# Attention scores computed in one tile mode, with the mask moved out of the memory queries' matmuls and the instruction order refitted

## Chip, cores, metric

One core of one Trainium2 chip. The metric is device time in microseconds (us) of one launch, lower is better. Runs of the kernel before on several chips lie between 2154 and 2166 us. Every run whose state is on record was in the fast state, so the comparisons below are of fast runs with fast runs.

## The reference

A sequence of 2048 tokens of width 576 goes through four residual layers: A (windowed attention, 32 heads of 18), B (32 heads of 128, segments of 32 tokens with 8 memory tokens that one segment hands to the next), then A and B again. The change touches B alone:

```python
for s in range(n_seg):                       # 64 segments of 32
    h = jnp.concatenate([mem, xs], axis=1)   # 8 memory rows, 32 x rows
    q, k, v = h @ Wq, h @ Wk, h @ Wv         # (cut: per head, 32 heads of 128)
    scores = jnp.einsum('bhqe,bhke->bhqk', q, k) * scale
    scores = jnp.where(mask, scores, -1e9)   # memory queries see all 40 keys;
                                             # x queries see memory and earlier x
    p = softmax(scores); o = p @ v; o = o @ Wo
    mem = o[:, :M]; outs.append(o[:, M:])
```

The memory makes each B layer a chain of 64 steps. The kernel runs the two B layers as two **lanes**, the second five steps behind the first, so that one step computes 80 rows: 32 x rows and 8 memory rows of each lane. The A layers' tiles of 64 tokens are fitted between.

## The kernel before

The program isn't written in the order in which it runs. Each piece of work is an operation with an engine, an estimated duration, a priority and its dependencies. A planner in the kernel simulates the engines with those durations and emits instructions in the order that it finds. Its settings (`PR`) were fitted to the durations beforehand. **New durations or settings mean a new order.** The planner also has a model of instruction fetch, with one constant time:

```python
    LAT = {"PE": 0.22, "ACT": 0.08, "DVE": 0.08, "POOL": 0.08, "SP": 2.8, "NONE": 0.0}
    SWITCH = 0.1                                    # a change of TensorE's tile mode
    PAGE, AHEAD, FETCH, POS = 256, 64, 4.1, 63
    ...                                             # (cut) in fetched(), at each block border:
                avail = max(avail, t0 + (t1 - t0) * (page - self.AHEAD - p0) / (p1 - p0)) + self.FETCH
```

A block of 256 instructions is taken to be asked for 320 instructions before it starts (64 before the block ahead of it), and to be usable 4.1 us later.

The scores of 16 heads, twice a step:

```python
            for v, msk in ((m, self.mask_m[:].unsqueeze(1).to_broadcast([P, 4, W80])),
                           (x, self.mask_x[:].unsqueeze(2).to_broadcast([P, 2, 4, 48]))):
                nc.tensor.matmul(v, lhsT=self.ident4[:], rhs=msk, start=True, stop=False, skip_group_check=True)
            for i in range(4):                      # memory queries: four heads side by side in column tiles
                for c in range(4):
                    h = heads[i][c]
                    nc.tensor.matmul(m[c * 32:(c + 1) * 32, i, :], lhsT=q(h, MC, 32), rhs=k(h, 0, W80), start=False, stop=True, ...)
            for l in range(2):                      # x queries of each lane
                for i in range(4):
                    for c in range(4 if on[l] else 0):
                        h = heads[i][c]
                        nc.tensor.matmul(x[c * 32:(c + 1) * 32, l, i, :], lhsT=q(h, XC[l], 32), rhs=k(h, KX[l], 48), start=False, ...)
```

The two mask matmuls use the full array, the scores four column tiles. After them come the softmax on VectorE, ScalarE and GpSimd (`amax`, `Exp`, `norm`, `mult`), the value products in row tiles (`pv`, 48 matmuls), and the output projection (`oproj`, 160 matmuls on the full array, in operations of 20).

The A layers' weights don't fit on the core beside B's. Tile by tile they are loaded again into a ring of buffers, by SyncE's DMA queue, up to 320 KB each:

```python
        def fetch(e):                               # in wload(); i >= 9: the A output weights
            dma(out=w.t[:, 0:5 * n], in_=self.strips[i][:, 0:5 * n])
```

## Time and profile before

| | before |
|---|---|
| time, median of 3 runs | 2161.72 us (2159.29 to 2165.41) |
| span of the profiled execution | 2165.8 us |
| TensorE busy | 2061.8 us, 95% |
| VectorE, ScalarE, GpSimd busy | 64%, 54%, 43% |
| ring loads | 488 of 320 KB, median 3.4 us from issue to landing; 244 of 160 KB, 3.9 us |
| instruction packets (16 KB, 256 instructions) | 472 |

Read it so: TensorE is nearly always busy and the others are not, so a change pays if it takes work from TensorE or closes holes between its matmuls. The prediction below shows the lines.

### The profile page before, as it was taken

The numbers are of one execution on the slowest core, as the hardware profiler recorded it, in microseconds if no ns is written. First come the engines' busy times: TensorE is split into PE (matmuls) and PEld (weight loads), VectorE is DVE, ScalarE is ACT, GpSimd is POOL, SyncE is SP. The second block draws the span as 40 slices with busy tenths as digits, with TensorE's granted clock in tenths as the row PEclk, the third lists the DMA queues.
The fourth block names the chain that finished last, engine by engine and source line by source line (L and its number), as shares of the span: only waits on it lengthen the run. The fifth ranks groups of instructions, "written<-read, shape, count | busy, mean of one in ns | idle before, by whom it ended". The sixth has DMA issues, their size and how long they took to land.

```text
span 2165.8 us, 132233 instructions
## 1 busy us (share of the span) xinstructions
PE 2061.8 (95%) x60441; PEld 1727.4 (80%) x60441; DVE 1392.3 (64%) x3525; ACT 1169.7 (54%) x2859; POOL 937.7 (43%) x1325
## 2 busy tenths in 40 slices
PE   2698999999999999999999999999999999999997
PEld 2476888888888888888888888888888888888876
DVE  4466766666666666666666666666666666765675
ACT  2244555555556555555555555555555555655543
POOL 3145444454444544445444454444445445442220
PEclk9799999999999999999999999999999999999999
DMA  9654334343344343334333343333344434332110
GB/s 324 184 155 138 119 108 122 120 131 118 120 125 125 115 128 119 122 119 130 120 115 119 121 135 111 123 122 117 115 132 127 121 112 130 118 119 92 59 57 10
DMA packets 158305, 265.11 MB, mean 122 GB/s; under 512 B 23464, under 2 KB 89904, under 8 KB 157616
## 3 DMA queue, kind: packets, MB, share of 16 engines
q1 hardware_dynamic: 152016, 237.38, 35.8%
q0 software_dynamic: 4576, 18.88, 2.5%
q8 instruction: 472, 7.73, 1.5%
q14 instruction: 89, 0.73, 0.1%
q10 hardware_dynamic: 1152, 0.39, 0.1%
HBM read 240.46 MB, written 16.12 MB: 118 GB/s over the span
## 4 chain that ended last, share of the span: by engine, by line
PE 92%; DMA 4%; DVE 1%; issue 1%; ACT 1%; SPq 0%; POOL 0%; ACTq 0%; POOLq 0%
PE r L833 28%; PE r L987 18%; PE r L880 17%; PE r L573 7%; PE r L836 6%; PE r L963 3%; PE r L683 2%; PE r L912 2%; PE r L473 2%; PE r L916 2%; PE r L647 1%; PE r L922 1%; DMA ring<-strip 1%; DMA ring<-in_A_wqkv_dram 1%; PE r L622 1%
## 5 line engine op out<-in xcount | busy, mean ns | idle before, releaser
L833 PE MATMUL r<-hT,wq 128*128 128x80 bf16 (+1 forms) x8832 | 660.0, 198 | 6.9 <-issue 3.0
L833 PE MATMUL r<-hT,wk 128*128 128x80 bf16 (+1 forms) x8832 | 662.5, 199 | 1.6 <-issue 1.5
L833 PEld LDWEIGHTS <-wq 128*128 128x128 bf16 x8832 | 499.9, 98 | 33.6 <-issue 23.7
L836 PE MATMUL r<-hT,wqk_r 128*128 128x160 bf16 (+1 forms) x2208 | 507.2, 230 | 0.2 <-issue 0.2
L275 ACT ACTIVATE qk<-r 128x480 bf16<-128x480 f32 (+3 forms) x659 | 345.7, 529 | 244.6 <-PE r L836 230.8
L833 PEld LDWEIGHTS <-wk 128*128 128x128 bf16 x8832 | 447.5, 99 | 2.2 <-issue 2.2
L987 PE MATMUL r<-OT,wo 128*128 128x80 bf16 (+1 forms) x11040 | 415.8, 200 | 16.7 <-issue 10.8
L987 PEld LDWEIGHTS <-wo 128*128 128x128 bf16 x11040 | 393.9, 99 | 32.6 <-issue 22.5
L880 PE MATMUL r<-wv,hT 128*32 128x512 bf16 x5376 | 354.5, 382 | 0.0
L282 POOL TENSOR_TENSOR big<-qT,kT 128x1024 bf16<-128x1024 bf16 x188 | 314.3, 1691 | 60.4 <-ACT kT L275 51.9
L282 POOL TENSOR_TENSOR ex<-ex,sum 128x384 bf16<-128x384 bf16 x137 | 116.7, 852 | 468.4 <-DVE sum L782 360.7
L282 POOL TENSOR_TENSOR big<-big 128x1280 bf16<-128x1280 bf16 (+1 forms) x61 | 123.0, 2016 | 422.2 <-DVE big L282 403.6
L880 PEld LDWEIGHTS <-hT 128*32 128x32 bf16 x6720 | 166.2, 96 | 127.1 <-issue 2.6
L275 ACT ACTIVATE V<-r 128x512 bf16<-128x512 f32 x301 | 179.6, 597 | 157.8 <-PE r L880 154.9
L771 DVE TENSOR_REDUCE nmx<-r 128x4 f32<-128x320 f32 (+1 forms) x276 | 143.2, 519 | 163.7 <-PE r L916 162.6
L836 PEld LDWEIGHTS <-wqk_r 128*128 128x128 bf16 x2208 | 219.7, 99 | 0.3 <-issue 0.3
L573 PE MATMUL r<-xn,ring 128*128 128x64 bf16 x4725 | 185.7, 194 | 23.1 <-DMA ring<-in_A_wqkv_dram 18.7
L573 PEld LDWEIGHTS <-ring 128*128 128x128 bf16 x4725 | 161.5, 98 | 44.4 <-DMA ring<-in_A_wqkv_dram 19.9
L275 ACT ACTIVATE OT<-r 128x320 bf16<-128x320 f32 (+1 forms) x375 | 137.5, 425 | 103.8 <-PE r L963 103.3
L275 ACT ACTIVATE big<-r 128x384 bf16<-128x384 f32 (+1 forms) x289 | 110.4, 443 | 88.8 <-issue 65.6
L772 DVE TENSOR_TENSOR r<-r,nmx 128x320 f32<-128x320 f32 (+1 forms) x276 | 147.2, 533 | 9.4
L880 PE MATMUL r<-wv_r,hT 128*32 128x512 bf16 x1344 | 133.4, 380 | 0.0
(150 smaller groups left out, 2906.3 us busy)
## 6 DMA issues: line engine op xcount, KB each, us to landing
ring<-strip SPq DMA_DIRECT2D x488, 320.0 KB, 3.4
ring<-strip SPq DMA_DIRECT2D x244, 160.0 KB, 3.9
x1T<-x SPq DMA_DIRECT2D x32, 160.0 KB, 4.4
x<-x1T SPq DMA_DIRECT2D x32, 160.0 KB, 4.3
x3T<-x SPq DMA_DIRECT2D x32, 160.0 KB, 4.4
x<-x3T SPq DMA_DIRECT2D x32, 160.0 KB, 4.3
wo<-in_B_Wo_dram POOLq DMA_DIRECT2D x4, 1152.0 KB, 30.6
wq<-in_B_Wq_dram POOLq DMA_DIRECT2D x2, 2048.0 KB, 20.6
```

What stands on the lines that cost most here:

```text
L275: nc.scalar.activation(out=out, in_=in_, func=ACT.Copy, scale=1.0 if scale is None else scale)
L282: (self.nc.vector if e == "DVE" else self.nc.gpsimd).tensor_tensor(out=out, in0=in0, in1=in1, op=op)
L473: nc.tensor.matmul(psf, lhsT=(self.ones if c < 4 else self.ones_h)[:, :], rhs=xs.t[:, c].rearrange("p a t -> p (a t)"), start=(c == 0), st ...
L573: nc.tensor.matmul(ps.t[:, c * T:(c + 1) * T], lhsT=view()[:, kc, w0:w0 + P], rhs=xn.t[:, kc, :], start=(kc == 0), stop=(kc == 4))
L683: nc.tensor.matmul(ps.t[:, mb * T:(mb + 1) * T], lhsT=view()[:, c, w0:w0 + P], rhs=oT.t[:, c, :], start=(c == 0), stop=(c == 4))
L771: nc.vector.tensor_reduce(out=m, in_=v, axis=AX.X, op=ALU.max, negate=True)
L772: nc.vector.tensor_tensor(out=v, in0=v, in1=m.unsqueeze(len(shp) - 1).to_broadcast(shp), op=ALU.add)
L833: nc.tensor.matmul(pv[:, hh, wi, a:b], lhsT=self.Wb[wi][0][:, kc, h * P:(h + 1) * P], rhs=hT.t[:, kc, a:b], start=(hh == 0 and wi == 0 and ...
L836: nc.tensor.matmul(pv[:, hh, :, a:b], lhsT=self.Wb[0][1][:, h * P:(h + 1) * P], rhs=hT.t[:, 4:6, a:b], start=False, stop=(hh == n - 1), sk ...
L880: nc.tensor.matmul(ps.t[c * 32:(c + 1) * 32, :], lhsT=l, rhs=w, start=(kc == 0), stop=(kc == 4))
L963: nc.tensor.matmul(ps[c].t[:, i * n + a - c0:i * n + z - c0], lhsT=V[b].t[q4, r, i, :], rhs=pt.t[q4, i, b, a:z], start=(i == 0 and b == bl ...
L987: nc.tensor.matmul(psY.t[:, mb * W80 + c0:mb * W80 + c1], lhsT=self.wo[:, w0:w0 + P], rhs=self.OT[:, h % 16 // 4 * 8 + h // 16 * 4 + h % 4 ...
```

## The change

**Intent.** Keep the scores block in one tile mode. The memory queries get no mask: each query sees the keys of both lanes, and after the softmax's sums the reciprocal of the other lane's sum is set to zero by a multiply with an ownership table. The x queries' mask, now on 40 keys instead of 48, is added by four column-tiled matmuls. Then durations and settings were fitted again, which gives a new order of the whole program. The core of the diff:

```diff
-KX = (0, 32)
+KX = (0, 40)
+KL = SEG + NM
...
-        self.mask_m = mk = cp.tile([P, W80], BF16, name="mask_m")
+        self.own_m = om = cp.tile([P, 4, 2], F32, name="own_m")
+        nc.gpsimd.memset(om[0:32], 1.0)
+        self.sel(om[0:32, :, 0], [[0, 4]], -1, NM - 1, ALU.is_ge, 0.0)
+        self.sel(om[0:32, :, 1], [[0, 4]], 1, -NM, ALU.is_ge, 0.0)
...
             nc.vector.reciprocal(out=s, in_=s)
-        o = pl.op("DVE", 0.69, norm, prio, [o], acq=[ss], uses=[e_])
+            if acq:
+                nc.vector.tensor_tensor(out=s, in0=s, in1=self.own_m[:], op=ALU.mult)
+        o = pl.op("DVE", 0.87 if acq else 0.69, norm, prio, [o], acq=[ss], uses=[e_])
...
-                nc.tensor.matmul(v, lhsT=self.ident4[:], rhs=msk, start=True, stop=False, skip_group_check=True)
+            for c in range(4):
+                q4 = slice(c * 32, (c + 1) * 32)
+                v, msk = (own(x, c * 32, 32, 0, NM, SEG), own_x) if all(on) else (x[q4], mx.unsqueeze(2).to_broadcast([P, 2, 4, KL]))
+                nc.tensor.matmul(v, lhsT=self.ident[:, 0:32], rhs=msk, start=True, stop=False, skip_group_check=True)
...
-        o = pl.op("PE", 0.68 if all(on) else 0.56, mm, prio, [self.qk_ev[g] for g in gs], acq=[psm, psx, em, ex],
+        o = pl.op("PE", 0.5 if all(on) else 0.39, mm, prio, [self.qk_ev[g] for g in gs], acq=[psm, psx, em, ex],
...
-PR = dict(qk=0.388, qkd=0.053, v1=1.358, v0=0.674, w=-0.059, s0=0.001, s1=-1.032, p0=1.109, p1=-0.981, o=0.434,
+PR = dict(qk=(0.121, -0.204), qkd=(0.07, 0.15), v1=(3.035, 1.45), v0=(5.889, 14.703), s0=(-0.83, 0.204), s1=(-7.824, -0.786), p0=(-5.413,
```

Cut: the views on 320 columns, small corrections of other durations, and the rest of the settings (a pair of values for even and odd steps where there was one).

More of the change, by code (lines that the diff above doesn't have):

```diff
@@ L60 @@
     LAT = {"PE": 0.22, "ACT": 0.08, "DVE": 0.08, "POOL": 0.08, "SP": 2.8, "NONE": 0.0}
-    SWITCH = 0.1
+    SWITCH = 0.097
     PAGE, AHEAD, FETCH, POS = 256, 64, 4.1, 63
@@ L160, in run @@
                             continue
-                        if alt is not None and o.prio > alt.prio + PR["w"]:
+                        if alt is not None and o.prio > alt.prio + PR["w" + mode]:
                             skipped.append(it)
@@ L299, in setup @@
         self.sel(ident[:], [[-1, P]], 1, 0, ALU.is_equal, 0.0)
-        self.ident4 = ident4 = cp.tile([P, P], BF16, name="ident4")
         self.ones = ones = cp.tile([P, P], BF16, name="ones")
@@ L322, in setup @@
         self.sel(ma0[:], [[ADIL, AW], [1, 16]], 0, -HALO, ALU.is_ge, NEG)
-        self.mask_m = mk = cp.tile([P, W80], BF16, name="mask_m")
-        nc.gpsimd.memset(mk[:], 0.0)
-        self.sel(mk[:, 40:80], [[0, 40]], 1, -NM, ALU.is_ge, NEG)
-        self.sel(mk[:, 0:40], [[0, 40]], -1, NM - 1, ALU.is_ge, NEG)
-        self.sel(mk[:, 0:40], [[0, 40]], -1, 2 * NM - 1, ALU.is_ge, 0.0)
-        self.mask_x = mx = cp.tile([P, 2, 48], BF16, name="mask_x")
+        self.own_m = om = cp.tile([P, 4, 2], F32, name="own_m")
+        nc.gpsimd.memset(om[0:32], 1.0)
+        self.sel(om[0:32, :, 0], [[0, 4]], -1, NM - 1, ALU.is_ge, 0.0)
+        self.sel(om[0:32, :, 1], [[0, 4]], 1, -NM, ALU.is_ge, 0.0)
+        self.mask_x = mx = cp.tile([P, 2, KL], BF16, name="mask_x")
         nc.gpsimd.memset(mx[:], 0.0)
-        nc.gpsimd.memset(mx[:, 0, 40:48], NEG)
-        nc.gpsimd.memset(mx[:, 1, 0:8], NEG)
-        self.sel(mx[:, 0, 0:32], [[-1, SEG]], 1, 0, ALU.is_ge, NEG)
-        self.sel(mx[:, 1, 16:48], [[-1, SEG]], 1, 0, ALU.is_ge, NEG)
+        self.sel(mx[:, 0, 0:SEG], [[-1, SEG]], 1, 0, ALU.is_ge, NEG)
+        self.sel(mx[:, 1, NM:KL], [[-1, SEG]], 1, 0, ALU.is_ge, NEG)
         self.Wb = []
@@ L397, in setup @@
         nc.vector.memset(wo[:, 11 * 1280:12 * 1280], 0.0)
-        nc.vector.tensor_copy(out=ident4[:].rearrange("p (a b) -> p a b", a=4), in_=ident[:, 0:32].unsqueeze(1).to_broadcast([P, 4, 32]))
         nc.vector.memset(mem0T[:], 0.0)
@@ L403, in setup @@
             nc.vector.tensor_copy(out=epadT[q4 * AH:(q4 + 1) * AH], in_=et)
+            nc.vector.tensor_copy(out=self.own_m[q4 * 32:(q4 + 1) * 32], in_=self.own_m[0:32])
         pp = self.pool("psum", 1, space=PSUM)
@@ L526, in pr @@
             return due - span * (1.0 - f)
-        Q = PR["A"]
+        Q = PR[f"A{layer}"]
         if layer == 1:
@@ L567, in a_tile @@
                     n = 256 if c < 4 else P
-                    view, w, ow = self.wload(part * 3 + c // 2, self.A_wqkv, (P, 512), part * D + CB[c], n, pr(Q[1]) - PR["ring"], wgate)
+                    view, w, ow = self.wload(part * 3 + c // 2, self.A_wqkv, (P, 512), part * D + CB[c], n, pr(Q[1]) - PR[f"ring{layer}"], wgate)
                 w0 = c % 2 * CB[1]
@@ L574, in mm @@
                                          start=(kc == 0), stop=(kc == 4))
-                o = pl.op("PE", 0.15, mm, pr(Q[1] + 0.03 * part), [o, ow], acq=[ps, dst[part]] if c == 0 else (),
+                o = pl.op("PE", 0.146, mm, pr(Q[1] + 0.03 * part), [o, ow], acq=[ps, dst[part]] if c == 0 else (),
                           uses=[xn, *w] if c == 0 else [xn, *w, ps], lat=0.0 if c < 4 else None, mm=5)
@@ L623, in logits @@
                                      start=(c == 0), stop=(c == 4))
-        o = o_l = pl.op("PE", 0.4, logits, pr(Q[3]), [o], acq=[psL, e_], uses=[big], mode="C", mm=20)
+        o = o_l = pl.op("PE", 0.29, logits, pr(Q[3]), [o], acq=[psL, e_], uses=[big], mode="C", mm=20)
         def amax(e):
@@ L652, in a_tile @@
             ps = [pl.buf("r") for _ in range(NQ)]
-            b = pl.op("PE", 0.09 * nb, lambda e, ps=ps, c0=c0, nb=nb: spread(ps, c0, nb), pr(Q[4] + 0.02 * n), [b], acq=ps,
+            b = pl.op("PE", 0.03 + 0.05 * nb, lambda e, ps=ps, c0=c0, nb=nb: spread(ps, c0, nb), pr(Q[4] + 0.02 * n), [b], acq=ps,
                       uses=[e_], mode="R", mm=4 * nb)
@@ L677, in a_tile @@
                 n = 256 if mb < 4 else P
-                view, w, ow = self.wload(9 + mb // 2, self.A_wo, (CB[1], CB[4]), mb * P, n, pr(Q[6]) - PR["ring"], o_l)
+                view, w, ow = self.wload(9 + mb // 2, self.A_wo, (CB[1], CB[4]), mb * P, n, pr(Q[6]) - PR[f"ring{layer}"], o_l)
             w0 = mb % 2 * P
@@ L683, in mm @@
                     nc.tensor.matmul(ps.t[:, mb * T:(mb + 1) * T], lhsT=view()[:, c, w0:w0 + P], rhs=oT.t[:, c, :], start=(c == 0), stop=(c == 4))
-            o = pl.op("PE", 0.15, mm, pr(Q[6]), [o, ow], acq=[ps] if mb == 0 else (),
+            o = pl.op("PE", 0.147, mm, pr(Q[6]), [o, ow], acq=[ps] if mb == 0 else (),
                       uses=[oT, *w] if mb == 0 else [oT, *w, ps], lat=0.0 if mb < 4 else None, mm=5)
@@ L797, in load_x @@
         self.hT[t] = hT
-        gate = pl.op("NONE", 0.0, None, t - 0.42, [self.qk_op.get(t - 1)], acq=[hT])
+        gate = pl.op("NONE", 0.0, None, t + PR["lx"], [self.qk_op.get(t - 1)], acq=[hT])
         self.x_in[t] = {l: gate for l in range(2)}
@@ L807, in load_x @@
                                     lambda e, l=l, s=s, xnb=xnb: self.copy(e, hT.t[:, :, XC[l]:XC[l] + SEG], xnb.t[:, s % NS]),
-                                    t - 0.42, [dep, gate], uses=[hT, xnb])
+                                    t + PR["lx"], [dep, gate], uses=[hT, xnb])
             if l == 0 and t % 2 == 0:
@@ L811, in load_x @@
                                      lambda e, s=s, xnb=xnb: self.copy(e, hT.t[:, :, W80:HW_], xnb.t[:, s % NS + 1, :, 0:HW_ - W80]),
-                                     t - 0.42, [dep, gate], uses=[hT, xnb])
+                                     t + PR["lx"], [dep, gate], uses=[hT, xnb])
             if s == 0:
@@ L837, in mm @@
                                  start=False, stop=(hh == n - 1), skip_group_check=True)
-        o = pl.op("PE", 0.0003 + (0.356 if b - a == W80 else 0.275) * n, mm, prio, [*self.x_in[t].values(), *self.mem_in[t]] + ([self.w_in[wi][n_] for wi in range(2) for n_ in
+        o = pl.op("PE", (0.356 if b - a == W80 else 0.275) * n, mm, prio, [*self.x_in[t].values(), *self.mem_in[t]] + ([self.w_in[wi][n_] for wi in range(2) for n_ in
                   {h // 16 for h in heads}] if t == 0 else []), acq=[ps, sb], uses=[hT], mm=9 * n)
@@ L880, in mm @@
                         nc.tensor.matmul(ps.t[c * 32:(c + 1) * 32, :], lhsT=l, rhs=w, start=(kc == 0), stop=(kc == 4))
-            o = pl.op("PE", 1.08, mm, prio, [gate] + (self.mem_in[t] if k == 1 else []) +
+            o = pl.op("PE", 1.075, mm, prio, [gate] + (self.mem_in[t] if k == 1 else []) +
                       ([self.w_in[2][r], self.vr_in] if t == 0 else []), acq=[ps], uses=[hT, V], mode="C", mm=20)
@@ L896, in vm, with own @@
         def vm(tile_):
-            return tile_[:, 0:320].rearrange("p (i k) -> p i k", i=4)
+            return tile_[:, 0:8 * KL].rearrange("p (i l k) -> p i l k", i=4, l=2)
         def vx(tile_):
-            return tile_[:, 0:384].rearrange("p (l i k) -> p l i k", l=2, i=4)
+            return tile_[:, 0:8 * KL].rearrange("p (l i k) -> p l i k", l=2, i=4)
+        def own(v, p0, pn, c0, dl, n):
+            f = v[p0:p0 + pn, 0, 0, c0:c0 + 1]
+            return bass.AP(f.tensor, f.offset, [list(f.ap[0]), [v.ap[1][0] + dl, 2], list(v.ap[2]), [1, n]])
         def mm(e):
@@ L909, in k @@
                 return qkt[h // 3].t[:, h % 3, 1, a:a + n]
-            for v, msk in ((m, self.mask_m[:].unsqueeze(1).to_broadcast([P, 4, W80])),
-                           (x, self.mask_x[:].unsqueeze(2).to_broadcast([P, 2, 4, 48]))):
-                nc.tensor.matmul(v, lhsT=self.ident4[:], rhs=msk, start=True, stop=False, skip_group_check=True)
+            mx = self.mask_x[:]
+            own_x = mx[:, 0:1, 0:SEG].unsqueeze(2).to_broadcast([P, 2, 4, SEG])
+            for c in range(4):
+                q4 = slice(c * 32, (c + 1) * 32)
+                v, msk = (own(x, c * 32, 32, 0, NM, SEG), own_x) if all(on) else (x[q4], mx.unsqueeze(2).to_broadcast([P, 2, 4, KL]))
+                nc.tensor.matmul(v, lhsT=self.ident[:, 0:32], rhs=msk, start=True, stop=False, skip_group_check=True)
             for i in range(4):
@@ L915, in mm @@
                     h = heads[i][c]
-                    nc.tensor.matmul(m[c * 32:(c + 1) * 32, i, :], lhsT=q(h, MC, 32), rhs=k(h, 0, W80), start=False, stop=True,
+                    nc.tensor.matmul(m[c * 32:(c + 1) * 32, i], lhsT=q(h, MC, 32), rhs=k(h, 0, W80), start=(i == 0), stop=True,
                                      skip_group_check=True)
@@ L921, in mm @@
                         h = heads[i][c]
-                        nc.tensor.matmul(x[c * 32:(c + 1) * 32, l, i, :], lhsT=q(h, XC[l], 32), rhs=k(h, KX[l], 48), start=False,
+                        nc.tensor.matmul(x[c * 32:(c + 1) * 32, l, i, :], lhsT=q(h, XC[l], 32), rhs=k(h, KX[l], KL), start=False,
                                          stop=True, skip_group_check=True)
-        o = pl.op("PE", 0.68 if all(on) else 0.56, mm, prio, [self.qk_ev[g] for g in gs], acq=[psm, psx, em, ex],
-                  uses=[qkt[g] for g in gs], mode="C", mm=50 if all(on) else 34)
-        a = self.softmax(t, psm, em, 320, prio, o, "DVE", vm, lambda x: x[:, :, 16:96], lambda x: x[:, :, k0:k0 + 96],
+        o = pl.op("PE", 0.5 if all(on) else 0.39, mm, prio, [self.qk_ev[g] for g in gs], acq=[psm, psx, em, ex],
+                  uses=[qkt[g] for g in gs], mode="C", mm=52 if all(on) else 36)
+        a = self.softmax(t, psm, em, 320, prio, o, "DVE", vm, lambda x: x[:, :, 16:96].rearrange("p i (l k) -> p i l k", l=2), lambda x: x[:, :, k0:k0 + 96],
                          lambda x: x[:, :, :, MC:MC + 32], 384, pt, True)
@@ L932, in tout @@
             return bass.AP(f.tensor, f.offset, [list(f.ap[0]), [W80 + XC[1], 2], [3 * W80, 4], [W80, 2], [1, 32]])
-        a = self.softmax(t, psx, ex, 384, prio + 0.02, o, "POOL", vx, lambda x: x[:, :, :, 16:64],
+        a = self.softmax(t, psx, ex, 8 * KL, prio + 0.02, o, "POOL", vx, lambda x: own(x, 0, P, 16, NM, KL),
                          lambda x: x[:, :, :, k0:k0 + 64].rearrange("p l i (b q) -> p l i b q", q=32), tout, 512, pt, False, a)
@@ L964, in mm @@
                                          start=(i == 0 and b == blocks[0]), stop=(i == 3 and b == blocks[-1]), skip_group_check=True)
-        o = pl.op("PE", 0.45 if n == W80 else 0.3, mm, prio, [dep] + self.v_done(t, r), acq=ps, uses=[pt, *V.values()], mode="R",
+        o = pl.op("PE", 0.4 if n == W80 else 0.3, mm, prio, [dep] + self.v_done(t, r), acq=ps, uses=[pt, *V.values()], mode="R",
                   mm=16 * len(blocks))
@@ L1030, in b_step @@
         self.qkt, self.qk_ev, self.PT, self.ot, self.o_ev = {}, {}, {}, {}, []
+        pr = {k: v[t % 2] for k, v in PR.items() if isinstance(v, tuple) and len(v) == 2}
         if t == 0:
@@ L1033, in b_step @@
         for g in range(11):
-            self.qk(t, g, t + PR["qk"] + PR["qkd"] * g)
-        self.vpass(t, 1, t + PR["v1"])
-        self.vpass(t, 0, t + PR["v0"])
+            self.qk(t, g, t + pr["qk"] + pr["qkd"] * g)
+        self.vpass(t, 1, t + pr["v1"])
+        self.vpass(t, 0, t + pr["v0"])
         for r in range(2):
-            self.scores(t, r, t + PR[f"s{r}"])
+            self.scores(t, r, t + pr[f"s{r}"])
         for r in range(2):
-            self.pv(t, r, t + PR[f"p{r}"])
-        dep = self.oproj(t, [t + PR["o"] + PR["od"] * k for k in range(8)])
+            self.pv(t, r, t + pr[f"p{r}"])
+        dep = self.oproj(t, [t + pr["o"] + pr["od"] * k for k in range(8)])
         if t + 1 < self.nsteps:
             self.load_x(t + 1)
-        self.mem_out(t, dep, t + PR["mo"])
-        self.x_out(t, dep, t + PR["xo"])
+        self.mem_out(t, dep, t + pr["mo"])
+        self.x_out(t, dep, t + pr["xo"])
         if t + 1 < self.nsteps:
-            self.vpass(t + 1, 2, t + PR["v2"])
+            self.vpass(t + 1, 2, t + pr["v2"])
     def run(self):
@@ L1087 @@
 DLY = 5
-PR = dict(qk=0.388, qkd=0.053, v1=1.358, v0=0.674, w=-0.059, s0=0.001, s1=-1.032, p0=1.109, p1=-0.981, o=0.434,
-          od=0.001, mo=0.162, xo=1.055, v2=2.128, a1=2.228, a1s=1.336, a2=0.453, a2s=7.821, fin=5.91, res=-5.123,
-          ring=-6.622, A=(-0.03, 0.482, 0.785, 0.737, 0.843, -0.012, 0.929, 0.994))
+PR = dict(qk=(0.121, -0.204), qkd=(0.07, 0.15), v1=(3.035, 1.45), v0=(5.889, 14.703), s0=(-0.83, 0.204), s1=(-7.824, -0.786), p0=(-5.413,
+          -0.051), p1=(-2.211, -0.302), o=(5.11, 2.006), od=(-1.932, -0.245), mo=(-6.487, -2.417), xo=(7.511, -1.007), v2=(3.475, 5.064),
+          wF=0.655, wC=-1.375, wR=-11.269, a1=2.707, a1s=0.139, a2=1.312, a2s=6.823, fin=11.546, res=-17.789, ring1=0.582, ring3=1.682,
+          lx=0.997, rr=-6.665, A1=(-12.517, -0.219, -2.406, 1.974, -4.644, -3.501, -0.646, 2.439), A3=(-8.888, 0.558, -6.353, 2.082,
+          0.962, -2.769, 0.698, 0.288))
 LEAD = 5
```

## The prediction

> **What bounds the kernel now.** First the page's busy shares and 40 slices, then the chain.
>
> ```profile
> PE 2061.8 (95%) x60441; PEld 1727.4 (80%) x60441; DVE 1392.3 (64%) x3525; ACT 1169.7 (54%) x2859; POOL 937.7 (43%) x1325
> PE   2698999999999999999999999999999999999997
> PEclk9799999999999999999999999999999999999999
> PE 92%; DMA 4%; DVE 1%; issue 1%; ACT 1%; SPq 0%; POOL 0%; ACTq 0%; POOLq 0%
> ```
>
> TensorE is full from the fourth slice to the last but one, at full clock, and is 92% of the chain that ended last. No other engine is above 64%. So time leaves the kernel only as TensorE's own time: work, or holes between its matmuls. The first ~90 us are a DMA-bound start (the DMA 4%) that the change leaves alone. A busy sum overlaps pipelined matmuls, so I work with start-to-start times, read from the timeline of TensorE in a middle stretch:
>
> ```profile
> 1200.70 1.06 PE L880 MATMUL r<-wv,hT 128*32 128x512 bf16 x16
> 1201.57 0.41 PE L880 MATMUL r<-wv_r,hT 128*32 128x512 bf16 x4
> 1201.79 1.05 PE L880 MATMUL r<-wv,hT 128*32 128x512 bf16 x16
> ...
> 1209.73 3.22 PE L987 MATMUL r<-OT,wo 128*128 128x80 bf16 x85 [0.99 <-issue]
> ...
> 1223.13 0.23 PE L836 MATMUL r<-hT,wqk_r 128*128 128x160 bf16 x1
> 1223.21 0.30 PE L912 MATMUL r<-mask_m,ident 128*128 128x320 bf16 x1
> 1223.34 0.33 PE L912 MATMUL r<-mask_x,ident 128*128 128x384 bf16 x1
> 1223.60 0.33 PE L916 MATMUL r<-qk 128*32 128x80 bf16 x16
> 1223.75 0.43 PE L922 MATMUL r<-qk 128*32 128x48 bf16 x32
> 1224.00 1.06 PE L880 MATMUL r<-wv,hT 128*32 128x512 bf16 x16
> ...
> 1230.83 0.39 PE L880 MATMUL r<-wv_r,hT 128*32 128x512 bf16 x4
> 1231.15 0.31 PE L912 MATMUL r<-mask_m,ident 128*128 128x320 bf16 x1
> ```
>
> Read the left column. Four value matmuls into four column tiles take 0.22 us when the next ones are of the same mode (1201.57 to 1201.79), but 0.32 us when a full-array mask matmul follows (1230.83 to 1231.15): **a change of mode costs 0.10 us** (96 ns is the median difference over the records, whichever two of the three modes meet: full array, column tiles, row tiles). A scores block takes 1223.21 to 1224.00 = 0.79 us: masks 0.13 and 0.26 (0.16 of streaming and one change), memory scores 0.15, x scores 0.25. It runs 138 times:
>
> ```profile
> L912 PE MATMUL r<-mask_x,ident 128*128 128x384 bf16 x138 | 45.2, 327 | 0.0
> L912 PE MATMUL r<-mask_m,ident 128*128 128x320 bf16 x138 | 42.4, 307 | 0.0
> L771 DVE TENSOR_REDUCE nmx<-r 128x8 f32<-128x384 f32 x138 | 75.6, 548 | 0.0
> L771 DVE TENSOR_REDUCE nmx<-r 128x4 f32<-128x320 f32 x138 | 67.6, 490 | 163.7 <-PE r L916 162.6
> L282 POOL TENSOR_TENSOR ex<-ex,sum 128x384 bf16<-128x384 bf16 x137 | 116.7, 852 | 468.4 <-DVE sum L782 360.7
> ```
>
> These groups by form give the softmax's side of the same blocks; their idle time shows VectorE and GpSimd waiting for TensorE, not the reverse.
>
> **What the Trainium skill says.** "TensorEngine Tiling (Array Packing)", Key Properties: changing the tiling mode drains the engine, while tiles of one mode run independently. The trace agrees: 0.10 us per change, four 512-column matmuls in 0.22 us. "TensorE: Matmul & The Clock Gate", "Wait — 56ns, not 53.3ns?": start to start is N/2.4 GHz plus 2.5 ns, with a floor near 25 ns. The trace agrees with the first (216 ns for 512 columns); the x scores need 0.25 us for eight rounds of four, 31 ns a round, where 48 columns would stream in 22, so they sit at such a floor. "Runtime: NRT & Kernel Launch", Instruction fetch mechanics: instructions come in blocks of 256 and the fetch is mostly hidden. Here it is not quite: the page counts 472 instruction packets, and TensorE's "issue" holes, like the 0.99 us above, recur at multiples of 256 of its instructions. Holes above 0.15 us between 200 and 2090 us sum to about 27 us, nearly all of this kind.
>
> **The change part by part.**
> 1. *Masks.* Two full-array matmuls (0.144 + 0.160 us) become four column-tiled ones of 2x4x32 = 256 columns side by side: 256/2.4 + 2.5 = 109 ns by the skill's formula, as the value rows behave. 138 x (304 - 109) ns = **26.9 us off**.
> 2. *Mode changes.* The order of the two built programs (no times in it) has 1151 changes of mode before, 953 after. The 138 inside the scores blocks go; the other 60 come from the refitted plan and from blocks that now follow values without a change. In the steady two-step pattern I count 34 before, 28 after. 198 x 0.096 = **19.0 us off**.
> 3. *x scores on 40 keys instead of 48:* 3.3 ns of streaming a round, but the round is at its floor: 0, at the very most 3 us.
> 4. *552 more TensorE instructions* (four pairs for two, 138 times), 276 more matmuls: their time is in part 1; they add two blocks to fetch.
> 5. *Softmax.* x on 320 instead of 384: VectorE saves about 58 + 67 + 66 ns (the rows at 384 less those at 320) per block, GpSimd about 852/6 = 140, ScalarE 50. The ownership multiply adds a small VectorE operation, about 0.18 us (the 128x4 reciprocal's 178 ns), and the reciprocal grows by 25 ns. VectorE breaks even: +28 us and -26 us. None is on the path: in the steady pattern the second product with the values starts at least 0.9 us after its softmax is done.
> 6. *Refit.* The built order also moves work between engines: the 5x256 additions on VectorE go from 33 to 63 (825 ns each there, 2611 on GpSimd), some projection evictions follow them, and large output evictions go to ScalarE. I estimate VectorE at about +60 us, 1450 of 2110 us, or 69%. Ring loads for weights are no tighter but in one place: the last projection block to the output projection, about 4.4 us of work, against 3.4 to 3.9 us from issue to landing.
>
> Sum on TensorE: 26.9 + 19.0 = 46 us of work that has nothing beside it, so 2161.7 - 46 = 2116. Summing median start-to-start times over the whole of both orders gives -54, partly an artefact of averaging merged value blocks; I trust the 46 more and add 2. Fetch holes: over each block boundary I add up the durations of the 320 instructions ahead of it. In both orders about one position in six lies under 4.5 us (18% before, 16% after), where before shows its holes; shortfalls against 4.5 us sum to 22 and 16 us. So I credit 2 to 3 us. **2112 us**, 2.3% faster; the steady two steps go from about 62.6 to about 61.2 us.
>
> **The rivals.**
> *Fetch takes it back.* The same instructions in less time, and a fetch limit per block, could return some of the gain as longer "issue" holes. For it: the holes exist, and scores and value products are the densest stretches. Against: the count of dense windows does not grow. If true, 10 to 20 us come back: 2122 to 2132.
> *The softmax chain or VectorE becomes the bound.* The extra multiply lies on the memory queries' chain, and one slack is only 0.9 us. Against: the x half gets shorter by as much, the new order has about 8 us between scores and their last value product where the old had 6.8, and VectorE has 30% to spare. If true: waits of the value products for pt of 0.3 us in each step, 20 us: 2132.
> *Ring weights arrive late* at the one tight place: up to 0.5 us in 30 patterns, 15 us: 2127.
> *The refit is worth more than its count.* Its orders are more regular (whole projection blocks, fewer splits), and fetch and ring waits may all but vanish: 20 us more, 2092.
>
> **Range and chances.** The 46 us are counts times measured costs and should hold within 5. Holes and waits may move by 15 either way. So 2094 to 2130 for 8 in 10. The limit of 2% is 2118.5, only 6 us above my number and inside the rivals' reach: 0.67 faster, 0.32 the same, 0.01 slower.
>
> **What would show it.** Right if: the timeline shows four mask matmuls at 128*32 with about 0.11 us to the first memory score, a scores block of about 0.51 us behind values, x scores still 0.25 us; TensorE's busy share stays near 95%; VectorE near 1450 us; "issue" holes sum to about as before. Wrong if the mask matmuls run one after the other (0.4 us: parts 1 and most of 2 gone), if value products wait for pt, or if holes at block boundaries grow by 10 us or more.

## The result, and the profile after

| | before | after |
|---|---|---|
| time, median of 4 runs | 2160.51 us (2155.93 to 2165.41) | 2137.43 us (2130.64 to 2139.59) |
| ratio, 95% interval | | 0.9886 (0.9862 to 0.9911) |
| changes of mode in the order | 1151 | 953 |
| instruction packets | 472 | 474 |

A ratio is formed from the fast runs of both kernels, not from the medians above, so it isn't quite the ratio of these. Below, a ratio is turned into us with 2159 us for the kernel before. The change gives 1.1%, 25 us, where 2.3% and 50 us were predicted, and the time lies outside the predicted range.

From the page of the profiled execution after (first busy us, share and instructions, then the shares of the chain that ended last):

```profile
PE 2017.4 (95%) x60717; PEld 1732.3 (81%) x60717; DVE 1416.8 (66%) x3754; ACT 1137.8 (53%) x2803; POOL 832.5 (39%) x1289
...
PE 89%; DMA 6%; issue 2%; DVE 2%; ACT 1%; SPq 0%; ACTq 0%; DVEq 0%
```

TensorE's busy sum fell by 44 us, and its share stayed. TensorE is still the bound. "issue", time in which it waited for nothing that the profile shows, has gone from 1% to 2% of the chain. TensorE's timeline around one scores block of after (start in us, duration, engine, line, operation, operands, tile, shapes, count):

```profile
1210.65 0.39 PE L879 MATMUL r<-wv_r,hT 128*32 128x512 bf16 x4
1210.87 0.28 PE L919 MATMUL r<-mask_x,ident 128*32 128x256 bf16 x4
1210.98 0.32 PE L923 MATMUL r<-qk 128*32 128x80 bf16 x16
1211.12 0.42 PE L929 MATMUL r<-qk 128*32 128x40 bf16 x32
1211.37 0.84 PE L879 MATMUL r<-wv,hT 128*32 128x512 bf16 x12
```

The four masks run side by side: 0.11 us from the first to the first memory score. The memory scores take 0.14 and the x scores 0.25 us. Values follow at once, and the block takes 0.50 us where it took 0.79. So the block itself did what was intended. What has grown stands in the groups of the output projection (busy us, mean ns | idle just before it, and what ended most of that), before and after:

```profile
L987 PE MATMUL r<-OT,wo 128*128 128x80 bf16 (+1 forms) x11040 | 415.8, 200 | 16.7 <-issue 10.8 <-ACT OT L275 3.5 <-DVE OT L277 1.1
```

```profile
L994 PE MATMUL r<-OT,wo 128*128 128x80 bf16 (+1 forms) x11040 | 418.6, 200 | 27.6 <-issue 22.9 <-ACT OT L276 3.3 <-DVE OT L278 0.5
```

Same matmuls, 11 us more idle, all under "issue". These holes lie at fixed places. I counted TensorE's instructions (each matmul is two, a weight load and a multiply) and added up the excess of start-to-start times within six instructions of each multiple of 256. From 90 us on it is **35.0 us before and 51.1 us after**. I call these the border holes. TensorE's other idle time (gaps of over 0.15 us away from the borders) is 17 us in both. One caution: each profile is one execution, and the one of before took longer than any of the kernel's timed runs, at a clock (0.992) like theirs. A span is 1.7 us shorter than the time of its run, so a run at the median of before has 2158.8 us, and the profile's 2165.8 is 7 us more. The profile of after (2133.8) is typical.

The same half of a step in the two timelines shows how the order differs. After, with SyncE's queue of loads (SPq) beside TensorE:

```profile
1218.07 0.80 SPq L507 DMA_DIRECT2D ring<-strip  x2
1218.17 0.88 PE L994 MATMUL r<-OT,wo 128*128 128x80 bf16 x20
1219.26 0.58 PE L680 MATMUL r<-oT,ring 128*128 128x64 bf16 x5 [0.21 <-DMA ring<-strip]
1219.78 0.54 PE L970 MATMUL r<-pt,V 32*128 32x48 bf16 x48
1219.87 0.33 SPq L507 DMA_DIRECT2D ring<-strip  x1
1220.25 2.90 PE L994 MATMUL r<-OT,wo 128*128 128x80 bf16 x76
1223.57 1.03 PE L994 MATMUL r<-OT,wo 128*128 128x80 bf16 x24 [0.42 <-issue]
```

Before:

```profile
1175.81 0.54 PE L963 MATMUL r<-pt,V 32*128 32x48 bf16 x48
1176.29 1.18 PE L987 MATMUL r<-OT,wo 128*128 128x80 bf16 x20
1177.30 0.31 PE L683 MATMUL r<-oT,ring 128*128 128x64 bf16 x5
...
1178.48 2.33 PE L987 MATMUL r<-OT,wo 128*128 128x80 bf16 x60
1181.37 1.28 SPq L510 DMA_DIRECT2D ring<-strip  x3
```

After, three ring loads are issued at 1218.07 to 1219.87, and the value products and 100 projection matmuls in a row follow at 1219.78. Those 100 break after 76, with a hole of 0.42 us. Before, the same projection is split by other work, and the three loads come when it is over.

### The profile page after: what moved, and what is told of

Read it like the earlier page. It is cut to its first block, busy times and chain, and to the rows that moved or that the text cites. A ratio compares the mean times of both kernels' runs of the same rounds, so it can differ in the third digit from the quotient of the medians.

```text
span 2133.8 us, 132983 instructions
## 1 busy us (share of the span) xinstructions
PE 2017.4 (95%) x60717; PEld 1732.3 (81%) x60717; DVE 1416.8 (66%) x3754; ACT 1137.8 (53%) x2803; POOL 832.5 (39%) x1289
## 4 chain that ended last, share of the span: by engine, by line
PE 89%; DMA 6%; issue 2%; DVE 2%; ACT 1%; SPq 0%; ACTq 0%; DVEq 0%
PE r L832 29%; PE r L994 18%; PE r L879 17%; PE r L570 7%; PE r L835 7%; DMA ring<-strip 3%; PE r L970 3%; PE r L680 2%; PE r L644 2%; PE r L470 2%; PE r L929 1%; PE r L919 1%; DMA x<-in_B_mem_dram 1%; PE r L619 1%; PE r L923 1%
## 5 line engine op out<-in xcount | busy, mean ns | idle before, releaser
L276 ACT ACTIVATE qk<-r 128x480 bf16<-128x480 f32 (+2 forms) x668 | 351.0, 526 | 265.7 <-PE r L835 254.7
L994 PE MATMUL r<-OT,wo 128*128 128x80 bf16 (+1 forms) x11040 | 418.6, 200 | 27.6 <-issue 22.9
L283 POOL TENSOR_TENSOR ex<-ex,sum 128x320 bf16<-128x320 bf16 x138 | 106.9, 775 | 570.7 <-DVE sum L779 509.2
L879 PEld LDWEIGHTS <-hT 128*32 128x32 bf16 x6720 | 173.1, 96 | 127.8 <-issue 5.0
L768 DVE TENSOR_REDUCE nmx<-r 128x8 f32<-128x320 f32 x276 | 133.3, 483 | 108.6 <-PE r L923 108.4
L570 PE MATMUL r<-xn,ring 128*128 128x64 bf16 x4725 | 176.9, 194 | 15.6 <-DMA ring<-in_A_wqkv_dram 11.6
L276 ACT ACTIVATE big<-r 128x256 bf16<-128x256 f32 (+1 forms) x288 | 109.1, 430 | 89.4 <-PE r L644 88.4
L283 POOL TENSOR_TENSOR xnb<-x,st 128x256 bf16<-128x256 f32 x124 | 64.6, 521 | 205.4 <-DVE st L476 205.4
L1013 DVE CAST hT<-r 128x64 bf16<-128x64 f32 (+1 forms) x68 | 14.9, 219 | 194.9 <-PE r L994 194.8
L769 DVE TENSOR_TENSOR r<-r,nmx 128x320 f32<-128x320 f32 x276 | 137.8, 499 | 9.5
```

The lines of the kernel that those rows point to most:

```text
L276: nc.scalar.activation(out=out, in_=in_, func=ACT.Copy, scale=1.0 if scale is None else scale)
L283: (self.nc.vector if e == "DVE" else self.nc.gpsimd).tensor_tensor(out=out, in0=in0, in1=in1, op=op)
L570: nc.tensor.matmul(ps.t[:, c * T:(c + 1) * T], lhsT=view()[:, kc, w0:w0 + P], rhs=xn.t[:, kc, :], start=(kc == 0), stop=(kc == 4))
L768: nc.vector.tensor_reduce(out=m, in_=v, axis=AX.X, op=ALU.max, negate=True)
L769: nc.vector.tensor_tensor(out=v, in0=v, in1=m.unsqueeze(len(shp) - 1).to_broadcast(shp), op=ALU.add)
L879: nc.tensor.matmul(ps.t[c * 32:(c + 1) * 32, :], lhsT=l, rhs=w, start=(kc == 0), stop=(kc == 4))
```

## The experiments

**Theories.** *Loads delay the fetch*: the work went as counted; the refitted order starts ring loads just ahead of TensorE's densest stretch, the fetch of instructions, itself a DMA (queue q8 of the page), comes late beside them, and holes give back part of the gain. *Density alone*: the same instructions in less time meet a fixed fetch time more often, wherever the loads lie. *Less saved than counted*: the block's 27 us and the 19 us of mode changes weren't worth that. The expectations on record give theories letters; I go by these names.

### e1 and e2: one half of the change at a time

e1 is the new block with the settings and other durations of before, e2 the old block with those of after, the order made anew in both. Both give correct results.

```diff
 # e1, against after (and the other settings of before alike)
-    SWITCH = 0.097
+    SWITCH = 0.1
-                        if alt is not None and o.prio > alt.prio + PR["w" + mode]:
+                        if alt is not None and o.prio > alt.prio + PR["w"]:
```

```diff
 # e2, against before (and the other settings of after alike)
-        Q = PR["A"]
+        Q = PR[f"A{layer}"]
```

> Only the new scores block, with the plan settings of the kernel before (its order of operations is made anew with them: 1021 mode changes against 1151). Work saved by count: 138 x 0.195 us for the masks = 26.9 us and 130 x 0.096 = 12.5 us for mode changes, 39 us. Theory A (the work saved is as counted, and longer holes at instruction-block boundaries return part of it, because the same blocks are used up faster and meet other loads): 2125 to 2140 us, holes of TensorE with releaser 'issue' or at block boundaries grown by 5 to 20 us from about 25. Theory B (the refitted plan is what costs; the new block itself gives its count): 2118 to 2124 us, faster than the changed kernel by over 10 us, with holes as in the kernel before.

> Only the refitted plan settings and operation times, with the old scores block: 1180 mode changes against 1151, so 2.8 us more work. Theory A: no gain, 2160 to 2175 us, holes a little above those of before. Theory B (the refitted order costs by itself): 2175 to 2185 us, the 15 to 20 us that the changed kernel lacks.

Measured: e1 2281.56 us (ratio 1.058), e2 2236.54 us (1.0361), against 2157.98 us. Both are slower than either kernel, and no theory had that. The waits in e1's trace are of another sort (columns: us in total, times, longest us):

```profile
PE r L570 <- DMA ring<-strip: 33.2, 37, 2.5
PE r L470 <- ACT xs L464: 32.5, 31, 5.8
```

What follows: in both runs, settings used with durations that they weren't fitted to gave a poor order (e2 even has 1180 changes of mode), and in e1's TensorE waits for weights and for ScalarE. These runs say nothing about the two halves. To take them apart, the **order** must be held fixed, which e5 and e6 do.

### e3 and e4: both kernels without the traffic of the ring loads

Each ring load is cut to a corner of 2 KB. Results are wrong on purpose; TensorE's instructions and their order are untouched.

```diff
 # e3 against after, e4 against before
         def fetch(e):
-            dma(out=w.t[:, 0:5 * n], in_=self.strips[i][:, 0:5 * n])
+            dma(out=w.t[0:16, 0:64], in_=self.strips[i][0:16, 0:64])
```

> The changed kernel with the repeated weight loads into the ring cut from 320 KB to 2 KB each (wrong result on purpose, same instructions and order). The trace of the changed kernel shows an instruction block usable 4.1 us after its request in quiet stretches and 5.1 us where 0.7 to 1 MB of ring loads move meanwhile. Theory A: block-boundary holes fall from about 40 us to under 12, ring waits (7 us) vanish, time falls by 25 to 45 us to 2092 to 2112 us. Theory B (holes are not of the fetch, or the fetch does not depend on the loads): under 10 us, which are the ring waits.

> The kernel before with the same cut of ring loads (wrong result on purpose). Theory A: holes fall from about 25 us to under 10 and time by 15 to 25 us, to 2136 to 2146 us; then the change is worth nearly its count of 46 us between the two quiet kernels, ratio of the quiet pair 0.978 to 0.983 against 0.989 with the loads. Theory B: ratio of the quiet pair stays near 0.989.

Measured: e3 2084.71 us (0.966, interval 0.9646 to 0.9675), e4 2136.51 us (0.9901, 0.9886 to 0.9916). So the loads cost after (0.9886 - 0.966) x 2159 = 49 us and before 21 us. **Without them the change is worth 52 us**, 2136.51 - 2084.71, or 2.4%: what had been predicted for the whole. That is more than "Loads delay the fetch" had expected: e3 lies under its 2092 to 2112 us, and the ratio of the quiet pair is 0.976, not 0.978 to 0.983. Holes at block borders fall to 5.9 and 6.3 us, and the projection's "issue" to under 1 us. After (e3), then before (e4):

```profile
L994 PE MATMUL r<-OT,wo 128*128 128x80 bf16 (+1 forms) x11040 | 409.1, 200 | 4.9 <-ACT OT L276 3.3 <-issue 0.9 <-DVE OT L278 0.5
```

```profile
L987 PE MATMUL r<-OT,wo 128*128 128x80 bf16 (+1 forms) x11040 | 410.9, 200 | 6.2 <-ACT OT L275 3.8 <-DVE OT L277 1.1 <-issue 0.7
```

"Less saved than counted" falls: 46 us were counted, 52 are there. "Density alone" falls too, as e3 is denser than after and has no more such holes than e4. But the cut removes the traffic and the waits for the weights together, which e7 was to part. The traces part them as well, since after and e3 have the same matmuls in the same order. Set against e3 one by one, after's are 52 us longer from 90 us on. Of this, 43 us lie within six instructions of a border at matmuls that use no ring weights, and 11 us at matmuls that do (before against e4: 28 and 5 of 31 us).

### e5 and e6: block and order apart, with the order held fixed

In e5 the new block is emitted in the order of before, in e6 the old block in the order of after: the planner is given the durations that led to the other order. Both are correct.

```diff
 # e5, against after (the settings of before as in e1, and the durations of before for the changed operations)
-        o = pl.op("DVE", 0.32 + 0.00208 * n, amax, prio, [dep], acq=[nmx], uses=[ps])
+        np_ = 320 if acq else 384
+        o = pl.op("DVE", 0.32 + 0.00208 * np_, amax, prio, [dep], acq=[nmx], uses=[ps])
-        o = pl.op("DVE", 0.87 if acq else 0.69, norm, prio, [o], acq=[ss], uses=[e_])
+        o = pl.op("DVE", 0.69, norm, prio, [o], acq=[ss], uses=[e_])
```

```diff
 # e6, against before (the settings of after as in e2, and the durations of after)
+        np_ = 320
+        o = pl.op("DVE", 0.32 + 0.00208 * np_, amax, prio, [dep], acq=[nmx], uses=[ps])
-        o = pl.op("DVE", 0.69, norm, prio, [o], acq=[ss], uses=[e_])
+        o = pl.op("DVE", 0.87 if acq else 0.69, norm, prio, [o], acq=[ss], uses=[e_])
```

> The new scores block in the order of operations of the kernel before, held fixed (the plan is made with the old operation times, only what is emitted is new): 966 mode changes against 1151, so 26.9 + 185 x 0.096 = 44.7 us less work. Theory A1 (the shorter block itself brings the longer fetch holes: each instruction block of 256 is used up sooner and the two-step pattern is no longer a whole number of blocks): 2125 to 2138 us, holes at block boundaries 45 to 55 us. Theory A2 (the refitted order brings them, by where dense stretches and ring loads meet): 2110 to 2122 us, holes about 35 us as in the kernel before, faster than the changed kernel by 15 us or more.

> The old scores block in the order of operations of the changed kernel, held fixed: 1033 mode changes against 953, so 26.9 + 80 x 0.096 = 34.6 us more work than the changed kernel. Theory A1: holes fall back towards 35 us, about 2137 + 35 - 12 = 2160 us. Theory A2: holes stay at 45 to 55 us, 2168 to 2176 us, slower than the kernel before.

Measured: e5 2128.28 us (0.9848, 0.9834 to 0.9863), e6 2153.42 us (0.9972, 0.9962 to 0.9983, 20 runs). **The new block in the old order is faster than the change as made**: 33 us off instead of 25, so with the new block the refitted order costs about 8 us. That is rough, as the two intervals just touch (0.9863 and 0.9862). With the old block it gains 6 us, though it has 118 mode changes fewer (1151 to 1033), 11 us by count. The projection's groups, e5 and then e6:

```profile
L995 PE MATMUL r<-OT,wo 128*128 128x80 bf16 (+1 forms) x11040 | 418.0, 200 | 14.6 <-issue 7.9 <-ACT OT L276 3.8 <-DVE OT L278 1.1
```

```profile
L988 PE MATMUL r<-OT,wo 128*128 128x80 bf16 (+1 forms) x11040 | 416.5, 200 | 29.6 <-issue 24.2 <-ACT OT L275 3.6 <-ACT qT L275 0.8
```

In the projection the holes go with the order, not with the block: 10.8 and 7.9 us in the old order, 24.2 and 22.9 in the new one (e6's profile is its slowest run, 2163.41 us; after's is a typical one). Border holes over the whole are 35.3 us in e5 and 47.3 in e6, against 35.0 and 51.1. So the holes came out as theory A2, the order, had expected. The times did not: e5 lies above A2's 2110 to 2122 us and within A1's range, and e6 lies below both ranges. The block in the old order thus costs something too, which e8 measures.

### e7: the traffic without its use

e3, with a full-size copy of each strip into a scratch area behind each small load, on the same queue. Wrong on purpose.

```diff
             dma(out=w.t[0:16, 0:64], in_=self.strips[i][0:16, 0:64])
+            dma(out=self.waste[i][:, 0:5 * n], in_=self.strips[i][:, 0:5 * n])
```

> The quiet changed kernel (ring loads of 2 KB, wrong result on purpose) with the full-size loads issued beside them into a scratch place in device memory that nothing reads or waits for. Theory A (the loads cost time because instruction fetches queue among them): back to 2120 to 2140 us, block-boundary holes 30 us or more, though no weight is waited for. Theory B (what the loads cost is that TensorE waits for weights): stays at 2085 to 2095 us.

Measured: 2195.45 us (1.0176). The largest of TensorE's waits in its trace, besides those of the start:

```profile
PE r L572 <- DMA ring<-strip: 33.0, 36, 2.5
PE r L996 <- issue: 19.3, 22, 2.3
PE r L682 <- DMA ring<-strip: 15.2, 12, 2.0
```

The run is spoilt as a measure of time: small loads queue behind the copies, and 48 us of waits for the ring come in. It met neither expectation (2120 to 2140 and 2085 to 2095 us). One thing it does show. The projection's "issue" holes are back, from 0.9 to 19.3 us, and no wait for weights stands before those matmuls. Set against e3 matmul by matmul, 34 us come in at borders at matmuls that use no ring weights. But the copies also write to memory, which ring loads don't, so it's a hint rather than a proof.

### e8: new block, old order, no traffic

```diff
 # against e5: the same cut as in e3
-            dma(out=w.t[:, 0:5 * n], in_=self.strips[i][:, 0:5 * n])
+            dma(out=w.t[0:16, 0:64], in_=self.strips[i][0:16, 0:64])
```

> The new scores block in the fixed order of before, with quiet ring loads (wrong result on purpose). By count 2136.5 - 44.7 = 2092 us, if the block's worth is as counted; the 2084.7 us of the quiet changed kernel would then leave about 7 us to the refitted order. If the block is worth less than counted, over 2097 us.

Measured: 2095.85 us (0.9699, 0.9685 to 0.9714), wrong on purpose. With e3 and e4 this splits the quiet gain of 52 us: the block gives 41 us by the medians, 44 by the ratios (e3 and e4 ran on another chip), and the refitted order another 11 or 8. The count for the block in this order was 26.9 us of masks and 185 mode changes of 0.096 us, 44.7 us. For the order, 13 changes of mode are 1.2 us, and border holes, 12.0 us in e8 and 5.9 in e3, another 6. So the refitted order is the better one when nothing is loaded, and the worse one by 8 us when the ring is.

e8 also gives what the loads cost in each case, by the ratios: 21 us before, 32 in e5 (0.9848 - 0.9699), 49 after. **Of the 28 us more that they cost after, about 11 come with the new block in the old order, and about 17 with the refitted order.** The block's density costs a little even without loads: border holes are 12.0 us in e8 and 6.3 in e4.

### e9 and e10: the loads moved, the order kept

In e9, ring loads of the A output weights that would be issued between the start of an odd step's projection and the copy of the memory rows after it are held back until that copy. A 16-byte copy of those memory rows, put ahead of them in the queue, makes them wait. TensorE's order is that of after. e10 is the control: the small copies are there, but nothing is held. Both are correct.

```diff
 # e9, against after
         def fetch(e):
-            dma(out=w.t[:, 0:5 * n], in_=self.strips[i][:, 0:5 * n])
+            def go():
+                dma(out=w.t[:, 0:5 * n], in_=self.strips[i][:, 0:5 * n])
+            if self.defer and i >= 9:
+                self.pend.append(go)
+            else:
+                go()
...
             def mm(e, k=k):                         # in oproj()
+                if k == 0 and t % 2 == 1 and 8 <= t < self.NSEG - 2:
+                    self.defer = True
...
             nc.vector.tensor_copy(out=hT.t[64:128, 5, w], in_=y[0:64, 4, w])   # in mem_out()
+            if self.pend:
+                nc.sync.dma_start(out=self.guard_out[:, :], in_=hT.t[0:1, 0, MC:MC + NM])
+                for go in self.pend:
+                    go()
+            self.defer, self.pend = False, []
```

```diff
 # e10, against e9
             if self.defer and i >= 9:
-                self.pend.append(go)
-            else:
-                go()
+                self.pend.append(lambda: None)
+            go()
```

> The changed kernel with three ring loads per two steps (those that the refitted order lets start just before the output projection of 100 matmuls that follows the value products of the odd steps) held back until that projection's memory rows are copied out, by a 16-byte transfer that waits for them; same order on TensorE, correct result. The trace of the changed kernel has 13 us of holes in that projection, three loads issued within 4 us before it in every pattern, where the kernel before had none and under 2 us. Theory A2 (the refitted order loses by loads meeting dense stretches): these holes fall to under 4 us, time by 7 to 13 us to 2124 to 2131 us. Rival (the holes there come of the density of pv48 and o100 alone): no change within 3 us.

> Control: the same 16-byte transfers that wait for the memory rows, placed at the same point of the queue, but the ring loads not held back. All theories: as the changed kernel, 2133 to 2141 us; if the small transfers cost or gain something themselves, it shows here.

Measured in five rounds, against 2159.26 us: **e9 2123.88 us (0.9834, 0.9812 to 0.9857)**, e10 2132.69 us (0.9879, 0.9861 to 0.9897). The intervals are disjoint from each other by 0.0004 only, but e9 also lies below after's (0.9862 and up), and e10 does not; and no run of e9 is as slow as the fastest of e10 (2128.18 and 2128.20 us). e9 comes out at the edge of what A2 expected (2124 to 2131 us, holes under 4), outside the rival's 3 us. e9's timeline at the place shown above:

```profile
1205.48 0.54 PE L976 MATMUL r<-pt,V 32*128 32x48 bf16 x48
1205.96 3.81 PE L1002 MATMUL r<-OT,wo 128*128 128x80 bf16 x100
1210.05 0.24 SPq L1025 DMA_DIRECT2D guard_out<-hT  x1
1210.39 1.32 SPq L509 DMA_DIRECT2D ring<-strip  x3
```

All 100 projection matmuls now run without a break, and the three loads follow. The projection's groups, e9 and then e10:

```profile
L1002 PE MATMUL r<-OT,wo 128*128 128x80 bf16 (+1 forms) x11040 | 415.5, 200 | 15.1 <-issue 10.6 <-ACT OT L276 3.3 <-DVE OT L278 0.5
```

```profile
L1001 PE MATMUL r<-OT,wo 128*128 128x80 bf16 (+1 forms) x11040 | 419.2, 200 | 33.7 <-issue 28.6 <-ACT OT L276 3.6 <-DVE OT L278 0.5
```

Border holes are 33.0 us in e9 and 55.9 in e10. The order repeats every two steps. In the 24 repeats where loads were held back, the holes in these 100 matmuls are 13.0 us in after, 17.7 in e10 and 3.0 in e9. The profiled run is e9's fastest (2113.38 us) and e10's slowest (2140.74), so their holes differ by more than their typical times do: 10 us by the ratios, and 11 from after to e9. Between e10 and e9 nothing but the start of these loads was moved, so at this place their start is the cause. e9 is the best correct version, 1.7% faster than before.

### What a fetch takes, from the records

The queue of instruction fetches is in the traces. A hole at a block border ends about 1.4 us after the end of that block's packet, which itself takes about 1.0 us. For all 59 holes above 0.4 us in before and after it was 1.2 to 1.9 us, so these holes end with the packet. If I put the request at the start of the instruction 320 ahead of the block, no packet starts sooner than about 1 us after it (0.8 and 1.0 us at the least). The time from request to usable is then as follows (between 200 and 2030 us):

| | before | after |
|---|---|---|
| median, 90% | 4.53, 5.3 us | 4.65, 5.7 us |
| without ring traffic (e4, e3): median | 3.9 us | 4.0 us |
| under 50 KB of ring loads in the 3.5 us after the request: median | 4.37 us | 4.07 us |
| 700 KB to 1 MB of them: median | 4.93 us | 5.07 us |
| blocks with 700 KB to 1 MB | 91 of 409 | 129 of 419 |
| holes of these blocks | 7.7 us | 15.6 us |
| sum of (request to usable, less TensorE's time for the 320 instructions) where positive | 22.9 us | 37.7 us |
| border holes measured | 24.9 us | 39.1 us |

The last two rows agree within 2 us, so the holes are fetches that came late. The bytes in 3.5 us aren't all that sets a fetch time, as the two kernels differ by 0.3 us where little is loaded. To see which side grew, I paired every fetch time of one kernel with every window of the other (the time TensorE needs for 320 instructions) and took the mean: fetch times of before with windows of after give 33.5 us where before with before gives 30.2, and fetch times of after with windows of before give 50.3. So by this estimate the windows add 3 us and the fetch times some 20.

## Why the prediction was wrong

1. **The work: right.** "26.9 + 19.0 = 46 us of work that has nothing beside it". The quiet pair has 52 us, nearer to the -54 from start-to-start times that I had trusted less. Masks, scores block (0.50 us for "about 0.51"), mode changes (953), x scores unchanged at 0.25 us: all as written. From the groups by form of after, the 40 keys indeed give nothing (mean 183 ns, 187 before), the ownership multiply takes 196 ns where 0.18 us was estimated, and GpSimd's multiply 775 ns where 712 (852 less 140) was:

```profile
L781 DVE TENSOR_TENSOR sum<-sum,own_m 128x8 f32<-128x8 f32 x138 | 27.1, 196 | 4.8
L283 POOL TENSOR_TENSOR ex<-ex,sum 128x320 bf16<-128x320 bf16 x138 | 106.9, 775 | 570.7 <-DVE sum L779 509.2 <-ACT OT L276 36.4 <-ACT V L276 11.8
```

2. **Softmax off the path: right.** Value products wait 4.7 us in all for their probabilities, 6.9 before. VectorE's 1416.8 us lie under the estimated 1450, and it is no bound.
3. **Ring weights late: right that it is small.** TensorE's waits for ring loads are 7.0 us in all, 3.7 before.
4. **The fetch: the step that failed.** "In both orders about one position in six lies under 4.5 us ... So I credit 2 to 3 us". I took the fetch as one constant, read off before, and looked at the ring loads only as weights that might come late, not as traffic beside the fetch. With loads it isn't one constant: 4.0 us in the quiet runs, 5 us beside 700 KB or more. The term of the sum "add 2" (2 to 3 us fewer holes) was +16 us in the profiled pair, 35.0 to 51.1. 46 - 16 = 30 us are left, where the ratio gives 25; the rest is within what runs of one kernel differ by. By the times the term is larger: the change is worth 52 us without loads and 25 with them, so 27 us went. The prediction's own sign of being wrong, "if holes at block boundaries grow by 10 us or more", is what came.
5. **The rival "Fetch takes it back" named the effect** and nearly its size (10 to 20 us; 16 by the profiles, 27 by the times), but with a reason, "the same instructions in less time", that is the smaller part. Density is worth 3 us by the pairing, and the block in the old order loses about 11 of the 28 us. The larger part is the order, in which three loads start just before the value products and 100 projection matmuls: e5 without that order wins back 8 us, and e9 without those loads there 11, each less than half of what is missing. I had dismissed the rival because "the count of dense windows does not grow", which left the loads out of account.
6. **The refit**, credited for its 60 fewer mode changes, gains 8 to 11 us without loads and costs 8 us with them. Its planner has the same constant fetch time in it (4.1 us), so it can't tell the two orders apart by this. That this is why the fit chose it is only argued.

**What stays open.** Border holes in e9 are still 33.0 us. The second place where three loads meet a dense stretch is just ahead of A's projections, which need them at once; its holes are 9.1 us before, 10.4 after and 5.0 in e9, which doesn't hold those loads back; why they fell there I don't know. What would win back the other 16 us isn't shown. e5 ends 33 us below before where its quiet pair has 41 to 44, yet its profiled run has no more border holes than before's, and the spans of these two profiles differ by 40.5 us (2165.8 and 2125.3). Most of those 8 to 11 us can be placed by an estimate. The profile of before is 7 us over its typical span and e5's is typical, and nearly all that loads add lies at borders (matmul by matmul, 29 of 31 us from e4 to before and 24 of 30 from e8 to e5). If those 7 us lie there too, a typical run of before has some 28 us of border holes and e5 some 7 more. That is not shown: each profile is one run. How the fetch is delayed by a load (in the DMA engines or in memory) no run here tells.

## What to carry to other kernels

When TensorE is full, count its instructions: a hole at a multiple of 256 without a visible wait was a late instruction fetch here, and with large loads (700 KB to 1 MB in 3.5 us) the fetch took about 1 us longer than with none. Look for the same before blaming a wait. Here the saved work could be read off from counts, but a new order of the same work must be judged with the start of its loads beside its densest stretches. To learn what half of a change is worth under a planner, hold the order fixed; letting it plan again measures the planner.

## What the Trainium skill lacked or had wrong

- "Runtime: NRT & Kernel Launch", Instruction fetch mechanics, says that crossing a block border is "mostly hidden", and gives no time. In these runs the borders cost 33 to 56 us of some 2140 when large loads run beside, 6 to 12 when they don't. From the request (taken as 320 instructions ahead) to use it takes 4.0 us without ring loads and 5 us beside 700 KB to 1 MB of them.
- The same section gives TensorE room for 2048 instructions, but also says that the next block is fetched while the current one runs. No prefetch eight blocks deep is seen here: delays of 1 us show, at single borders. The packets' times fit a request 320 instructions ahead, which the section doesn't give.
- "TensorEngine Tiling (Array Packing)", Key Properties, says that a change of tiling mode drains the engine, without a number. It is 96 ns here, whichever two of the three modes meet.
- "TensorE: Matmul & The Clock Gate", "Wait — 56ns, not 53.3ns?", has a floor near 25 ns from start to start. For rounds of four column tiles, each with its own weights, it was 31 ns at 48 and at 40 columns alike (0.25 us for eight rounds).
